# A gate's column sums: one fp32 matmul per step becomes one fp32r matmul on the high and low parts

## Chip, cores, metric

The kernel runs on one core of one Trainium2 chip. The metric is device microseconds for one execution. Three runs of the kernel before took 1857.21, 1858.81 and 1859.02 us, so the median is 1858.81 us.

## The reference

An attention over packed keys feeds a dense MLP, and its output feeds a mixture of experts. The change lies in the gate of that last part, so this is the piece that has to be seen (2304 tokens, 512 features, 8 experts):

```python
logits = x @ w_gate
logits = logits - logits.max()
P = np.exp(logits)
for _ in range(8):
    P /= P.sum(1, keepdims=True) + 1e-09
    P /= P.sum(0, keepdims=True) + 1e-09
    P *= N / E
out = np.zeros((N, D), dtype=np.float32)
for e in range(E):
    h = np.maximum(x @ w1[e], 0.0)
    ye = h @ w2[e]
    out += P[:, e:e + 1] * ye
```

`P` has one row per token and one column per expert. Eight times over, each row is divided by its sum and then each column by its sum.

## The kernel before

**Stages.** The first part (to about 420 us) is attention and the dense MLP. Then come the experts. The tokens stand in three groups of 512, 768 and 1024. The first group (about 420 to 780 us) is worked out in 32 units, one per quarter of an expert's hidden layer. While it runs, the weights of all experts are loaded, split into a high and a low part, and written back to memory for the two later groups, which take the rest of the time.

**A unit** (`unit`, L804) makes seven products of six matmuls each (`product`, L754, 256 columns) in three PSUM banks X, Z and Y. Between the products ScalarE copies a bank out (L815, L823, L826) and VectorE adds it to another bank (L817, L830, L833). `evac` then takes a finished bank out in two halves: ScalarE the high part (L761), VectorE the low part (L762). The second layer's matmuls (L784, 512 columns) of earlier units stand between the products. The names `hh`, `psc`, `psy`, `s` are the hidden layer's parts, the product banks, the second layer's banks and the copies.

**Weights beside it.** VectorE forms sums of weight blocks (L145 to L148, tile `wt`), ScalarE rounds a block to fp32r (L176, tile `w`), GpSimd subtracts to get the low part (L177), and SyncE writes both out (L181).

**The gate in it.** All 2304 rows of `P` lie in one tile of 128 partitions by 18 by 8. `balance` does one half step per call, and is called at fixed places of units 2 to 7: the 16 half steps take from 453 to 511 us. A row half step (`rows_step`, L712) is four VectorE instructions (L714 to L717) that divide each row by its sum, and a fifth (L719) that adds up the 18 rows of each partition to `cs`, 128 by 8. A column half step (`cols_step`, L722) adds `cs` over the partitions by a matmul with a matrix of ones (L724, a full fp32 matmul), after which VectorE makes the reciprocal (L726, L727) and multiplies `P` by it (L728).

**What sets the order.** The engines each run their own list of instructions strictly in order. The code is recorded in the order in which it is written, and a scheduler then orders each engine's list when the program is built, by durations that it assumes. So added or removed instructions can move others on the same engine. The matmul of a column step takes its PSUM bank from the four banks of the product banks (`ybank`, tag "c").

**Memory.** The tile pool `gc` holds the gate's small tiles. It is opened on the right side of the on-chip memory just before the pools of `s`, of half of `hb` (the second layer's operands of odd batches) and of `hh`, which are stacked next to it.

Of the kernel before, what the change touches and what calls it, by code (L numbers as in the profile page):

```python
# [10 lines left out]
F32 = mybir.dt.float32  # L11
F32R = mybir.dt.float32r
I32, U32, I64 = mybir.dt.int32, mybir.dt.uint32, mybir.dt.int64
AF = mybir.ActivationFunctionType
ALU = mybir.AluOpType
AX = mybir.AxisListType
# [3 lines left out]
T = B * S  # L20
DM, FF = 512, 2048
E, F = 8, 1024
# [10 lines left out]
EPS = 1e-9  # L33
# [5 lines left out]
def kernel(ctx: ExitStack, tc: tile.TileContext, qT, kT, v, pT,  # L39
                                     win, wout, wg, w1, w2, out):  # L40
    nc = tc.nc
# [14 lines left out]
    def pool(name, **kw):  # L56
        st, p = open_pool(name, **kw)
        ctx.push(st)
        return p

    const = pool("const", side="left")
# [13 lines left out]

    ident = const.tile([128, 128], F32, name="ident")
    make_identity(nc, ident)
    ones = const.tile([128, 128], F32, name="ones")
    nc.gpsimd.memset(ones, 1.0)


# [546 lines left out]
    for i, (f, c) in enumerate(seq):  # L628
        if i < 3:
            continue  # L630
        k = c + len(THIRDS) - len(BLOCKS[f])
# [45 lines left out]
    gc = pool("gc", side="right")  # L677
# [9 lines left out]
    def ybank():  # L687
        return psm.tile([128, 512], F32, tag="c", name="psy", bufs=4)
# [23 lines left out]
    def rows_step():  # L712
        rs = gc.tile([128, NT, 1], F32, tag="rs", name="rs")
        nc.vector.tensor_reduce(rs, P, axis=AX.X, op=ALU.add)  # L714
        nc.vector.tensor_scalar_add(rs, rs, EPS)
        nc.vector.reciprocal(rs, rs)
        nc.vector.tensor_tensor(P, P, rs.to_broadcast([128, NT, E]), op=ALU.mult)  # L717
        cs = gc.tile([128, E], F32, tag="cs", name="cs")
        nc.vector.tensor_reduce(cs, P.rearrange("p t e -> p e t"), axis=AX.X, op=ALU.add)  # L719
        return cs  # L720

    def cols_step(cs):  # L722
        ps = ybank()[:, :E]
        nc.tensor.matmul(ps, ones, cs, start=True, stop=True)  # L724
        cr = gc.tile([128, 1, E], F32, tag="cr", name="cr")
        nc.vector.tensor_scalar(cr[:, 0, :], ps, EPS, float(E) / T, op0=ALU.add, op1=ALU.mult)  # L726
        nc.vector.reciprocal(cr, cr)  # L727
        nc.vector.tensor_tensor(P, P, cr.to_broadcast([128, NT, E]), op=ALU.mult)  # L728

# [2 lines left out]
    def balance():  # L732

        n = steps["n"]
        if 0 <= n < 16:
            steps["n"] += 1
            if n % 2 == 0:
                steps["cs"] = rows_step()
            else:
                cols_step(steps["cs"])  # L740
# [510 lines left out]
```

## Time and profile before

| | |
|---|---|
| median of 3 runs | 1858.81 us |
| profiled execution, own time | 1860.79 us |
| its span, first to last instruction | 1858.9 us |
| PE busy | 1837.6 us (99%) |
| VectorE (DVE) busy | 1279.4 us (69%) |
| ScalarE (ACT) busy | 829.4 us (45%) |
| GpSimd (POOL) busy | 1047.0 us (56%) |
| mean granted clock of TensorE | 0.999 |

The profile comes from one execution, 1.98 us above the median of the runs; of that execution's own time, 1.9 us lie outside the span. PE is TensorE's matmuls, PEld its weight loads, which overlap the matmuls. Busy time of a matmul includes its way through the array, so PE can be called busy while one matmul follows another with a small hole. A fp32 matmul appears as two records, an fp32r matmul as one.

### The profile page before, as it was taken

How to read it: one execution, taken by the hardware profiler on the slowest of the kernel's cores; microseconds unless marked ns; L12 is line 12 of the kernel's file. 1: busy time of each engine (PE TensorE's matmuls, PEld its weight loads, DVE VectorE, ACT ScalarE, POOL GpSimd, SP SyncE). 2: the span in 40 equal slices, each digit the busy share in tenths (PEclk: the TensorE clock that was granted, in tenths of full speed). 3: DMA queues.
4: the chain of work that ended last, by engine and by line, in shares of the span. 5: the costliest groups of instructions: out<-in, count | busy, mean ns of one | idle time of the engine just before them, and what ended most of it. 6: DMA issues, size and time to landing. Idle time of an engine off the chain costs nothing.

```text
span 1858.9 us, 28526 instructions
## 1 busy us (share of the span) xinstructions
PE 1837.6 (99%) x10190; PEld 1663.2 (89%) x10190; DVE 1279.4 (69%) x2097; ACT 829.4 (45%) x1538; POOL 1047.0 (56%) x653
## 2 busy tenths in 40 slices
PE   8999999999999999999999999999999999999999
PEld 7899999998888898888888888888889999999998
DVE  4777777766766555588778877888775666666665
ACT  6667654644555555343333433333334323332323
POOL 3313322435688777278778777778764444444444
PEclk9999999999999999999999999999999999999999
DMA  7402211206789887767777787776788777788874
GB/s 277 159 27 77 69 46 47 103 2 229 252 317 325 299 271 255 243 219 257 234 249 233 233 267 233 238 238 228 248 307 268 276 258 266 258 245 265 267 251 148
DMA packets 166124, 403.55 MB, mean 217 GB/s; under 512 B 14192, under 2 KB 79712, under 8 KB 165984
## 3 DMA queue, kind: packets, MB, share of 16 engines
q1 hardware_dynamic: 131520, 346.15, 55.1%
q10 hardware_dynamic: 34464, 55.58, 9.8%
q8 instruction: 81, 1.33, 0.3%
q14 instruction: 59, 0.48, 0.1%
HBM read 273.96 MB, written 127.72 MB: 216 GB/s over the span
## 4 chain that ended last, share of the span: by engine, by line
PE 91%; DVE 3%; DMA 2%; issue 1%; ACT 1%; POOL 1%; SPq 0%; ACTq 0%; POOLq 0%; DVEq 0%
PE psc L754 35%; PE psx L1141 16%; PE psz L1141 12%; PE psy L430 11%; PE psy L784 7%; PE psh L411 6%; PE psh L364 1%; PE pp L270 1%; DMA raw<-win 1%; POOL w L177 1%; DMA raw<-w 1%; PE s L304 0%; PE s L238 0%; ACT w L176 0%; DMA kt<-kT 0%
## 5 line engine op out<-in xcount | busy, mean ns | idle before, releaser
L754 PE MATMUL psc<-xc,w 128*128 128x256 f32 (+2 forms) x4032 | 777.4, 335 | 2.3 <-ACT s L823 1.6
L754 PEld LDWEIGHTS psc<-xc,w 128*128 128x128 f32 x4032 | 666.3, 188 | 67.5 <-ACT s L823 1.8
L1117 POOL TENSOR_TENSOR hh<-hb,hh 128x1024 fp32r<-128x1024 f32 (+1 forms) x224 | 504.6, 2257 | 372.1 <-ACT hh L1116 314.4
L1116 ACT ACTIVATE hh<-hb 128x1024 fp32r<-128x1024 f32 (+1 forms) x224 | 213.8, 955 | 447.8 <-DVE hb L1114 197.8
L1141 PE MATMUL psx<-hh,wa 128*128 128x512 f32 (+1 forms) x1536 | 352.7, 362 | 0.0
L1141 PEld LDWEIGHTS psx<-hh,wa 128*128 128x128 f32 x1536 | 278.9, 188 | 30.2 <-ACT hh L1116 0.4
L1141 PE MATMUL psz<-hh,wa 128*128 128x512 f32 (+1 forms) x1152 | 261.9, 362 | 0.3 <-issue 0.3
L1141 PEld LDWEIGHTS psz<-hh,wa 128*128 128x128 f32 x1152 | 209.0, 188 | 23.2 <-issue 0.9
L430 PE MATMUL psy<-h,w 128*128 128x320 f32 (+2 forms) x1200 | 224.8, 331 | 0.2
L784 PE MATMUL psy<-w,hh 128*128 128x512 f32 x768 | 201.5, 395 | 3.9 <-ACT hh L761 3.3
L177 POOL TENSOR_TENSOR w<-raw,w 128x512 fp32r<-128x512 f32 (+1 forms) x128 | 157.9, 1255 | 76.9 <-ACT w L176 66.0
L1149 DVE TENSOR_TENSOR acc<-psx,acc 128x512 f32<-128x512 f32 (+1 forms) x248 | 152.1, 618 | 70.2 <-PE psx L1141 69.0
L430 PEld LDWEIGHTS psy<-h,w 128*128 128x128 f32 x1200 | 189.0, 188 | 12.2 <-ACT x L436 0.7
L1149 DVE TENSOR_TENSOR acc<-psz,acc 128x512 f32<-128x512 f32 (+1 forms) x184 | 112.6, 618 | 93.1 <-PE psz L1141 93.0
L1047 DVE SCALAR_TENSOR_TENSOR hb<-psc,gate 128x512 f32<-128x512 f32 (+1 forms) x256 | 157.3, 620 | 12.2 <-PE psc L754 7.3
L1021 POOL TENSOR_TENSOR wa<-rb,wa 128x512 fp32r<-128x512 f32 x80 | 132.6, 1666 | 49.9 <-ACT wa L1020 39.5
L784 PEld LDWEIGHTS psy<-w,hh 128*128 128x128 f32 x768 | 135.1, 189 | 27.8 <-ACT hh L761 4.6
L1114 DVE TENSOR_TENSOR hb<-hb 128x1024 f32<-128x1024 f32 (+1 forms) x96 | 133.5, 1390 | 28.9 <-POOL hh L1117 28.0
L411 PE MATMUL psh<-at,g 128*128 128x320 f32 (+2 forms) x768 | 123.4, 297 | 0.2 <-DVE r L417 0.2
L411 PEld LDWEIGHTS psh<-at,g 128*128 128x128 f32 x768 | 110.9, 189 | 4.3 <-DVE r L417 0.4
L177 POOL TENSOR_TENSOR w<-wt,w 128x512 fp32r<-128x512 f32 x64 | 83.7, 1316 | 47.8 <-ACT w L176 35.9
L129 POOL TENSOR_TENSOR ca<-ca,cc 128x512 int32<-128x512 int32 x28 | 36.7, 1311 | 102.6 <-ACT cc L128 94.1
(155 smaller groups left out, 1843.3 us busy)
## 6 DMA issues: line engine op xcount, KB each, us to landing
w<-kept_w SPq DMA_DIRECT2D x184, 512.0 KB, 4.8
kept_w<-wa SPq DMA_DIRECT2D x112, 512.0 KB, 4.6
wa<-kept_w SPq DMA_DIRECT2D x112, 512.0 KB, 4.8
kept_w<-w SPq DMA_DIRECT2D x96, 512.0 KB, 4.7
raw<-w ACTq DMA_DIRECT2D x58, 512.0 KB, 5.2
rb<-w ACTq DMA_DIRECT2D x64, 256.0 KB, 4.5
w<-kept_w SPq DMA_DIRECT2D x61, 256.0 KB, 4.3
raw<-win SPq DMA_DIRECT2D x16, 512.0 KB, 3.9
```

Of the source, the lines that this page charges most:

```text
L177: nc.gpsimd.tensor_tensor(w[:, 1, :n], t, w[:, 0, :n].bitcast(F32), op=ALU.subtract)
L411: nc.tensor.matmul(ps[:, u - begin:w - begin], gw[:, x, m * 128:(m + 1) * 128], at[:, y, g, u - b * S:w - b * S], start=(i == 0), stop=(i ...
L430: nc.tensor.matmul(ps[:, :n], w[:, x, d * 128:(d + 1) * 128], h[:, y, :], start=(i == 0), stop=(i == 11))
L754: last = nc.tensor.matmul(ps[:, :N], w[:, u, o + k * 128:o + (k + 1) * 128], x[v][:, k, :], start=(start and k + u + v == 0), stop=(k == 1 ...
L784: nc.tensor.matmul(ps, h[:, x, o:o + 128], w[:, y, :], start=(n % 4 + m + x + y == 0), stop=(n % 4 == 3 and m == 1 and x == 1), skip_group ...
L1021: nc.gpsimd.tensor_tensor(w[:, 1], src, w[:, 0].bitcast(F32), op=ALU.subtract)
L1047: nc.vector.scalar_tensor_tensor(HB[q][m, t][:, nn, :], src, 0.0, GATE[p, g // 4][:, t * N:(t + 1) * N], op0=ALU.max, op1=ALU.mult)
L1114: nc.vector.tensor_tensor(src, src, hb[MINUS[k]], op=ALU.subtract)
L1116: nc.scalar.activation(hi, src, AF.Copy)
L1117: nc.gpsimd.tensor_tensor(lo, src, hi.bitcast(F32), op=ALU.subtract)
L1141: nc.tensor.matmul(ps, A2[q, k][:, u, nn, d * 128:(d + 1) * 128], OPS[7 * q + k][v][:, nn, :], start=(first and nn + u + v == 0), stop=(nn ...
L1149: nc.vector.tensor_tensor(a, ps, a, op=ALU.add)
```

## The change

The eight sums of a partition are now split on ScalarE and VectorE into a part rounded to fp32r and the rest, side by side as 16 columns. One fp32r matmul with the same matrix of ones, now held as fp32r, adds both over the partitions. VectorE adds the two halves of the result as it takes them out of PSUM, and applies the constants in an instruction of its own.

```diff
@@ const @@
-    ones = const.tile([128, 128], F32, name="ones")
+    ones_r = const.tile([128, 128], F32R, name="ones")
+    ones = ones_r.bitcast(F32)
     nc.gpsimd.memset(ones, 1.0)
@@ rows_step, cols_step @@
         nc.vector.tensor_reduce(cs, P.rearrange("p t e -> p e t"), axis=AX.X, op=ALU.add)
-        return cs
-
-    def cols_step(cs):
-        ps = ybank()[:, :E]
-        nc.tensor.matmul(ps, ones, cs, start=True, stop=True)
+        parts = gc.tile([128, 2, E], F32R, tag="csr", name="parts")
+        nc.scalar.activation(parts[:, 0, :], cs, AF.Copy)
+        nc.vector.tensor_tensor(parts[:, 1, :], cs, parts[:, 0, :].bitcast(F32), op=ALU.subtract)
+        return parts
+
+    def cols_step(parts):
+        ps = ybank()[:, :2 * E]
+        nc.tensor.matmul(ps, ones_r, parts.rearrange("p k e -> p (k e)"), start=True, stop=True)
         cr = gc.tile([128, 1, E], F32, tag="cr", name="cr")
-        nc.vector.tensor_scalar(cr[:, 0, :], ps, EPS, float(E) / T, op0=ALU.add, op1=ALU.mult)
+        nc.vector.tensor_reduce(cr[:, 0, :], ps.rearrange("p (k e) -> p e k", e=E), axis=AX.X, op=ALU.add)
+        nc.vector.tensor_scalar(cr[:, 0, :], cr[:, 0, :], EPS, float(E) / T, op0=ALU.add, op1=ALU.mult)
         nc.vector.reciprocal(cr, cr)
         nc.vector.tensor_tensor(P, P, cr.to_broadcast([128, NT, E]), op=ALU.mult)
```

In the changed file the lines behind the first edit have numbers higher by 1, those behind the second by 5: the product is L759 there, the second layer L789, the high parts L766, the low parts L767. The new lines are L722 (ScalarE copy), L723 (VectorE subtraction), L728 (matmul), L730 (reduction out of PSUM) and L731 (constants). The tile `parts` takes 64 bytes of each partition, so the pools of `s`, `hh` and the odd `hb` begin 64 bytes lower than before, at addresses that are multiples of 64 bytes and no longer of 128.

The scheduler's lists are the same for GpSimd and SyncE, and on the other three engines up to the first column step. Between the first column step and unit 8 some instructions stand in another order. Three places follow, each with the list before and the list now.

VectorE, second column step; before, from the sums `cs` (L719) on; `wt` are the weight sums, `psc` the product banks:

```order
L719 TENSOR_REDUCE cs<-P 128x8
L145 TENSOR_TENSOR wt<-raw 128x256
L147 TENSOR_TENSOR wt<-raw 128x256
L830 TENSOR_TENSOR psc<-psc,s 128x256
L146 TENSOR_TENSOR wt<-wt,raw 128x256
L833 TENSOR_TENSOR psc<-psc,s 128x256
L148 TENSOR_TENSOR wt<-raw,wt 128x256
L762 SCALAR_TENSOR_TENSOR hh<-psc,hh 128x256 x2
L726 TENSOR_SCALAR cr<-psy 128x8
```

And now, where `parts` is the new tile:

```order
L720 TENSOR_REDUCE cs<-P 128x8
L835 TENSOR_TENSOR psc<-psc,s 128x256
L723 TENSOR_TENSOR parts<-cs,parts 128x8
L146 TENSOR_TENSOR wt<-raw 128x256
L148 TENSOR_TENSOR wt<-raw 128x256
L838 TENSOR_TENSOR psc<-psc,s 128x256
L147 TENSOR_TENSOR wt<-wt,raw 128x256
L767 SCALAR_TENSOR_TENSOR hh<-psc,hh 128x256
L149 TENSOR_TENSOR wt<-raw,wt 128x256
L767 SCALAR_TENSOR_TENSOR hh<-psc,hh 128x256
L730 TENSOR_REDUCE cr<-psy 128x8
L731 TENSOR_SCALAR cr<-cr 128x8
```

The addition into bank Z (L830, now L835) moved ahead of the first two weight sums, the subtraction stands behind it, and the addition into bank Y (L833, now L838) keeps its two weight sums in front.

ScalarE, third column step, before; `acc` is the copy of the second layer's first result:

```order
L790 ACTIVATE acc_4854<-psy 128x512 x2
L761 ACTIVATE hh<-psc 128x256
L111 DMA raw<-w 128x1024
L790 ACTIVATE acc_4854<-psy 128x512 x2
L823 ACTIVATE s<-psc 128x256
```

And now:

```order
L795 ACTIVATE acc_4854<-psy 128x512 x2
L766 ACTIVATE hh<-psc 128x256
L112 DMA raw<-w 128x1024
L722 ACTIVATE parts<-cs 128x8
L795 ACTIVATE acc_4854<-psy 128x512 x2
L828 ACTIVATE s<-psc 128x256
```

The new copy of `cs` stands behind two `acc` copies, a high part and the issue of a weight load; nothing else moved here.

TensorE, fourth column step, before; `xc_4182` holds the operands of the products behind which L830 and L833 come, `xc_4365` that of the unit's last product:

```order
L754 MATMUL psc<-xc_4182,w 128x256 x12
L784 MATMUL psy<-w,hh 128x512 x4
L754 MATMUL psc<-xc_4365,w 128x256 x6
L784 MATMUL psy<-w,hh 128x512 x14
L724 MATMUL psy<-cs,ones 128x8
L754 MATMUL psc<-xc_4181,w 128x256 x12
```

And now:

```order
L759 MATMUL psc<-xc_4182,w 128x256 x12
L759 MATMUL psc<-xc_4365,w 128x256 x6
L789 MATMUL psy<-w,hh 128x512 x18
L728 MATMUL psy<-parts,ones 128x16
L759 MATMUL psc<-xc_4181,w 128x256 x12
```

Four second-layer matmuls moved behind the unit's last product, which therefore follows at once on the product before it.

## Rows read from the trace of the kernel before

**Rows 1.** The page: busy time by engine; chain that ended last, by engine:

```profile
PE 1837.6 (99%) x10190; PEld 1663.2 (89%) x10190; DVE 1279.4 (69%) x2097; ACT 829.4 (45%) x1538; POOL 1047.0 (56%) x653
...
PE 91%; DVE 3%; DMA 2%; issue 1%; ACT 1%; POOL 1%; SPq 0%; ACTq 0%; POOLq 0%; DVEq 0%
```

**Rows 2.** Busy time of a window; waits of PE in it (us, times, longest):

```profile
453.00:512.00 59.00, 57.92 (x362) 51.64 (x362) 42.52 (x121) 30.00 (x72) 35.15 (x30) 1.00 0.70 249
...
PE psy L784 <- ACT hh L761: 0.9, 4, 0.3
```

**Rows 3.** Group by line, 453 to 512 us: xcount | busy, mean ns | idle:

```profile
L726 DVE TENSOR_SCALAR cr<-psy 128x8 f32<-128x8 f32 x8 | 1.3, 163 | 4.8 <-PE psy L724 4.8
```

**Rows 4.** Timeline, third column step: start us, us, engine, line [idle]:

```profile
468.74 1.53 PE L784 MATMUL psy<-w,hh 128*128 128x512 f32 x6
...
469.97 0.38 ACT L761 ACTIVATE hh<-psc 128x256 fp32r<-128x256 f32 x1
470.11 0.88 PE L754 MATMUL psc<-xc,w 128*128 128x256 f32 x6
...
470.38 0.42 DVE L762 SCALAR_TENSOR_TENSOR hh<-psc,hh 128x256 fp32r<-128x256 f32 x1 [1.41 <-ACT hh L761]
...
470.83 0.29 PE L724 MATMUL psy<-cs,ones 128*128 128x8 f32 x2
...
470.97 0.96 PE L754 MATMUL psc<-xc,w 128*128 128x256 f32 x6
```

**Rows 5.** Four small instructions by line: duration ns min/median/max, place:

```profile
L707 ACT ACTIVATE gm<-psy x1: 171/171/171, 447.4 to 447.4; 128x1 f32<-128x1 f32 x1
...
L701 DVE TENSOR_REDUCE grow<-psy x1: 278/278/278, 444.4 to 444.4; 1x1 f32<-1x128 f32 x1
...
L715 DVE TENSOR_SCALAR rs<-rs x8: 176/195/1260, 453.5 to 506.0; 128x18 f32<-128x18 f32 x8
...
L717 DVE TENSOR_TENSOR P<-P,rs x8: 307/494/1332, 455.1 to 506.5; 128x144 f32<-128x144 f32 x8
```

**Rows 6.** Timeline, first column step:

```profile
454.94 2.60 POOL L177 TENSOR_TENSOR w<-raw,w 128x512 fp32r<-128x512 f32 x2 [0.25 <-ACT w L176]
455.06 1.33 DVE L717 TENSOR_TENSOR P<-P,rs 128x144 f32<-128x144 f32 x1
...
456.65 0.40 DVE L719 TENSOR_REDUCE cs<-P 128x8 f32<-128x144 f32 x1
...
457.35 0.28 PE L724 MATMUL psy<-cs,ones 128*128 128x8 f32 x2
...
459.28 0.43 DVE L817 TENSOR_TENSOR psc<-psc,s 128x256 f32<-128x256 f32 x1 [0.86 <-PE psc L754]
```

**Rows 7.** Timeline, second column step:

```profile
461.68 0.44 DVE L719 TENSOR_REDUCE cs<-P 128x8 f32<-128x144 f32 x1
461.83 1.60 PE L754 MATMUL psc<-xc,w 128*128 128x256 f32 x12
462.82 0.43 DVE L830 TENSOR_TENSOR psc<-psc,s 128x256 f32<-128x256 f32 x1
463.27 0.29 PE L724 MATMUL psy<-cs,ones 128*128 128x8 f32 x2
463.72 1.20 PE L784 MATMUL psy<-w,hh 128*128 128x512 f32 x4 [0.17 <-ACT hh L761]
```

**Rows 8.** Timeline, fourth column step:

```profile
476.20 4.57 POOL L177 TENSOR_TENSOR w<-raw,w 128x256 fp32r<-128x256 f32 x4
...
478.62 0.44 DVE L719 TENSOR_REDUCE cs<-P 128x8 f32<-128x144 f32 x1
480.01 0.28 PE L724 MATMUL psy<-cs,ones 128*128 128x8 f32 x2
```

**Rows 9.** Weight loads and matmuls by line: duration ns min/median/max:

```profile
L500 PEld LDWEIGHTS pslg<-lx,wgs x56: 187/188/192, 361.2 to 418.0; 128*128 128x128 f32 x56
L1141 PE MATMUL psx<-hh,wa x1536: 333/389/497, 785.8 to 1853.6; 128*128 128x512 f32 x96, 128*128 128x384 f32 x96
```

## The prediction

> **What bounds the kernel now.** I read four things in this order: the page, the window in which the gate's steps run, the waits in it, and the timeline around single steps. The page says that TensorE (PE) is busy 99% of the span and makes up 91% of the chain that ended last [rows 1]. So a microsecond taken from or added to PE's list is one of the whole, unless a wait further on swallows it. In the window of the gate, 453 to 512 us, PE is busy 57.92 of 59.00 us, VectorE (DVE) 42.52, ScalarE 30.00 and GpSimd 35.15; the only wait of PE that is listed there is 0.9 us in four places, for ScalarE's high parts L761 [rows 2]. The gate's own instructions hide: VectorE's L726 waits for the matmul, 4.8 us in all [rows 3], but no row has PE waiting for the gate. To price the change I need what its matmul costs PE, and how long before that matmul its input is ready.
>
> **What the matmul costs now.** In the third step L724 starts at 470.83 and the next product at 470.97, so 0.14 us go to the two records of the fp32 matmul. The six products behind it take 0.96 us where the six before took 0.88 [rows 4], another 0.08. Together 0.22 us a step. In five of the eight steps (the first, third, fourth, sixth and seventh) a product follows like this, and the 0.22 us are PE's. In the other three the next instruction is a second-layer matmul that waits for ScalarE anyway: in the second step L724 starts at 463.27 and L784 at 463.72 with an idle 0.17 before it [rows 7]. Of these 0.45 us only 0.14 are the matmul's, so 0.31 us of slack swallow any saving.
>
> **What it costs then.** One fp32r matmul of 16 columns with its weight load is not in this trace. The nearest row is a product of 256 columns: twelve take 1.60 us [rows 7] and six 0.88 [rows 4], so six more cost 0.72 and one costs 0.12. From below the price is nothing, from above it is today's 0.22, if it goes through the array twice all the same. I take 0.12, the row's. The gain is 5 x 0.10 = 0.50 us, between 0 and 5 x 0.22 = 1.1.
>
> **What the longer way to it costs.** Between the sums `cs` and the matmul now stand a ScalarE copy and a VectorE subtraction. Neither is in the trace at this size. The nearest are a ScalarE copy of one column, 0.171 us [rows 5], and VectorE's L726 with 8 columns, 0.163 [rows 3]. A hand-over takes 0.03 (L761 ends at 470.35, L762 starts at 470.38 [rows 4]); I take that for all three. So the way is 0.17 + 0.17 + 0.09 = 0.43 us where both engines are free, and no less. What it does depends on the lead of today's `cs` on L724 and on what is queued ahead:
>
> - First step: `cs` ends at 457.05, L724 starts at 457.35 [rows 6]. The lead is 0.30, so PE waits at least 0.13. The subtraction would start at 457.28. GpSimd runs two subtractions from 454.94 for 2.60 us [rows 6], the second until 457.54. That holds VectorE back as GpSimd's run just before held L717 (1.33 us at 455.06, where 0.307 is its best [rows 5]): the matmul comes at 457.54 + 0.17 + 0.03 = 457.74 and the wait is 0.39. I take 0.39.
> - Second step, and alike the fifth and eighth: the lead is 463.27 - 462.12 = 1.15 us [rows 7], but the subtraction now stands behind the addition into Z (L830). That one needs the first six of the twelve products from 461.83, hence 461.83 + 0.88 + 0.03 = 462.74 at the earliest. With its 0.43 and the subtraction's 0.17 the matmul comes at 463.37, 0.10 late, inside the 0.31 us of slack above. The high part that L784 waits for comes no later, since L830 does not. Price 0. What is late next is the addition into Y behind two weight sums; the unit's last product needs its bank, and stands behind four second-layer matmuls that begin at 463.72 and take 1.20 us, which covers it.
> - Third step: the copy stands behind the high part L761, which ends at 470.35, the subtraction behind L762, which ends at 470.80; so the matmul comes at 471.03 instead of 470.83 [rows 4], 0.20 late. For the sixth step I take the same 0.20, though its matmul now stands behind more second-layer work, which could make it 0.
> - Fourth and seventh: the lead is 480.01 - 479.06 = 0.95 us. GpSimd's four subtractions from 476.20 take 4.57 us, 1.14 each [rows 8], so the third ends at 479.63. Held until then, the subtraction lets the matmul start at 479.83, before 480.01. Price 0.
>
> The waits add up to 0.39 + 2 x 0.20 = 0.79 us.
>
> **What comes behind the matmul.** L726 read PSUM and applied the constants in 0.16 us. Now a reduction out of PSUM (the nearest, L701, took 0.278) and the constants (L715, alike, 0.176 at the least) do it [rows 5]: 0.28 + 0.18 + 0.03 - 0.16 = 0.33 us more on VectorE per step. Behind it stands the addition L817, which today waits 0.86 us for PE [rows 6]. So even 0.39 + 0.33 is covered in the first step. In total VectorE gets 8 x (0.17 + 0.33) = 4.0 us more, against 59.00 - 42.52 = 16.5 us of idle time in the window [rows 2]. ScalarE gets 8 x 0.17 = 1.4 of its 29.0 idle us. No DMA is added; the weight loads that ScalarE issues move back by no more than a copy.
>
> [...] VectorE's L717, with both inputs in the on-chip memory, takes 0.307 us at best, 0.494 in the median and 1.332 at worst [rows 5]; the worst is the one that starts at 455.06 while GpSimd works from 454.94 [rows 6]. [...]
>
> **The sum.** -0.50 + 0.79 = +0.3 us. The profiled execution took 1860.79 us for a span of 1858.9, 1.98 above the median 1858.81. The difference holds for either, so I forecast 1858.81 + 0.3 = 1859.1 us. About 0.2% (3.7 us) is what a measurement of this kernel can tell from no change, so this is no change. Its own range goes from all gain and no wait, with the 1.08 us in which PE is idle in the window gone through the new order, 1858.81 - 1.1 - 1.1 = 1856.6, up to 1862.
>
> **Rivals.**
>
> *Slower through the lists.* Copy and subtraction stand at fixed places in lists that run in order: an evacuation ahead of them holds the matmul, and behind a late matmul PE has all its products. In the fourth step the unit's last product now follows at once on the one before it; it adds into a bank that VectorE must have read first (L833), and four second-layer matmuls no longer cover that. If PE waits for one more evacuation of 0.42 us [rows 4] in each step, that is 8 x 0.42 = 3.4 us. If GpSimd also holds VectorE in three of the eight by 1.332 - 0.307 = 1.02 us [rows 5], it is 6.5. The time is 1862.2 to 1865.3. It decides once PE stands 0.46 us per step on average. For it: GpSimd is busy 60% of the window. Against it: today PE waits 0.9 us in all here, and five of the leads can bear the longer way.
>
> *Slower or faster through addresses.* The 64 bytes of `parts` put the tiles `s`, `hh` and the odd `hb` on odd multiples of 64 bytes. All of the third part's L1141 matmuls stream `hh`. Weight loads show no difference: those of L500 read a tile whose slices begin on even and odd multiples of 64 by turns, and all take 187 to 192 ns [rows 9]. For streamed operands no row shows anything. [...] I put it at zero, the side of the row that was measured.
>
> *The matmul does not get cheaper.* If 16 columns in fp32r cost PE 0.22 us again, the gain of 0.50 goes and the time is 1859.6, still no change.
>
> *Faster.* If no wait appears, the new order removes PE's 1.08 us and the slack of 3 x 0.31 too, it is 1858.81 - 1.1 - 1.1 - 0.9 = 1855.7. Even that is within 0.2%, so faster needs addresses as well.
>
> **Chances.** The forecast with its own range 0.60, the matmul that costs the same 0.10, slower through the lists 0.15, slower through addresses 0.07, faster 0.08. So no change 0.70, slower 0.22, faster 0.08. The range leaves out the slow address case and the tails: 1856.0 to 1865.0.
>
> **What would show it.** Right: in the profile after, one record per step at L728, with about 0.12 us to the next product; a wait of PE before L728 of 0.2 to 0.4 us in the first and third step and none in the fourth and seventh; the rest of the span unchanged behind 540 us. Wrong: waits of PE before L728 or before the products of the fourth to sixth unit that add up to 3 us and more; or L1146 matmuls whose start-to-start time is no longer that of before, which would be the addresses.

## Result: 1.0% slower, and the profile after

The changed kernel takes 1876.62 us (median of 4 runs, 1875.41 to 1881.83); the kernel before took 1858.91 beside it. The ratio is 1.0103, 95% interval 1.0089 to 1.0116: 17.7 us slower. The forecast was 1859.1 with a range to 1865.0, so it was wrong. The profiled execution took 1881.83 us, its span is 1880.0.

The page after, answering [rows 1]:

```profile
PE 1855.4 (99%) x10182; PEld 1667.0 (89%) x10182; DVE 1294.6 (69%) x2113; ACT 832.0 (44%) x1546; POOL 1051.6 (56%) x653
...
PE 91%; DVE 4%; issue 1%; ACT 1%; POOL 1%; DMA 0%; ACTq 0%; POOLq 0%; DVEq 0%
```

PE has eight records less and 17.8 us more busy time: its matmuls got slower. Two rows say where. These are the matmuls by line (duration min/median/max, first and last start), of the kernel after; the column sums first:

```profile
L728 PE MATMUL psy<-parts,ones x8: 171/247/278, 461.1 to 517.5; 128*128 128x16 f32 x8
...
L1146 PE MATMUL psx<-hh,wa x1536: 331/392/504, 794.1 to 1874.7; 128*128 128x512 f32 x96, 128*128 128x384 f32 x96
```

And the column sums of the kernel before:

```profile
L724 PE MATMUL psy<-cs,ones x16: 170/215/256, 457.4 to 508.4; 128*128 128x8 f32 x16
```

From the first column sum to the last it took 51.0 us and takes 56.4: **+5.4 us in the gate**. From the first to the last matmul that streams `hh` into `psx` it took 1853.6 - 785.8 = 1067.8 us [rows 9] and takes 1080.6: **+12.8 us behind the gate**. Together 18.2, for 17.7 in the medians. The two spans differ by 21.1: another 3.7 us lie ahead of the first column sum (457.4 and 461.1), where the lists are the same and the granted clock from 440 to 450 us was 1.00 before and 0.83 after, and 0.8 are won back between the gate and the third part.

**In the gate**, the waits of PE from 455 to 545 us (total, times, longest), answering [rows 2], were 0.9 us for L761's high parts and little else. After:

```profile
PE psy L728 <- DVE parts L723: 2.3, 2, 1.7
PE psy L789 <- ACT hh L766: 0.6, 2, 0.3
PE psc L759 <- DVE psc L838: 0.5, 1, 0.5
PE psc L759 <- ACT s L828: 0.5, 1, 0.5
PE psy L789 <- DVE hh L767: 0.2, 1, 0.2
```

The longest is the third column step. The timeline after (start, duration, engine, line; idle before), from the second matmul on, answering [rows 4]:

```profile
467.22 0.25 PE L728 MATMUL psy<-parts,ones 128*128 128x16 f32 x1
...
469.21 2.55 POOL L178 TENSOR_TENSOR w<-wt,w 128x512 fp32r<-128x512 f32 x2 [8.17 <-ACT w L177]
469.33 0.16 DVE L730 TENSOR_REDUCE cr<-psy 128x8 f32<-128x16 f32 x1
469.53 1.00 DVE L731 TENSOR_SCALAR cr<-cr 128x8 f32<-128x8 f32 x1
...
470.80 1.12 DVE L733 TENSOR_TENSOR P<-P,cr 128x144 f32<-128x144 f32 x1
...
471.72 4.61 POOL L178 TENSOR_TENSOR w<-raw,w 128x256 fp32r<-128x256 f32 x4
...
472.50 1.32 DVE L716 TENSOR_SCALAR rs<-rs 128x18 f32<-128x18 f32 x1
...
474.36 0.85 DVE L718 TENSOR_TENSOR P<-P,rs 128x144 f32<-128x144 f32 x1
...
475.24 0.41 DVE L720 TENSOR_REDUCE cs<-P 128x8 f32<-128x144 f32 x1
...
475.92 0.43 DVE L723 TENSOR_TENSOR parts<-cs,parts 128x8 fp32r<-128x8 f32 x1
...
476.50 0.25 PE L728 MATMUL psy<-parts,ones 128*128 128x16 f32 x1 [1.73 <-DVE parts L723]
...
477.64 2.76 PE L789 MATMUL psy<-w,hh 128*128 128x512 f32 x6
```

The same instructions before, from the matmul at 463.27 [rows 7] on:

```profile
464.37 2.62 POOL L177 TENSOR_TENSOR w<-wt,w 128x512 fp32r<-128x512 f32 x2 [6.83 <-ACT w L176]
464.88 0.16 DVE L726 TENSOR_SCALAR cr<-psy 128x8 f32<-128x8 f32 x1
...
465.31 0.52 DVE L728 TENSOR_TENSOR P<-P,cr 128x144 f32<-128x144 f32 x1
...
466.83 0.19 DVE L715 TENSOR_SCALAR rs<-rs 128x18 f32<-128x18 f32 x1
...
467.36 0.49 DVE L717 TENSOR_TENSOR P<-P,rs 128x144 f32<-128x144 f32 x1
467.89 0.43 DVE L719 TENSOR_REDUCE cs<-P 128x8 f32<-128x144 f32 x1
```

Before, the sums were ready 5.05 us after the last matmul (463.27 to 468.32); after it is 8.43 (467.22 to 475.65). The new L731 takes 1.00 instead of nothing, beside GpSimd. All behind it slips against GpSimd's instructions, and L733, L716 and L718 now take 0.60, 1.13 and 0.36 longer beside them. These four add up to 3.1 of the 3.4 us. With copy and subtraction behind them the lead of 2.51 us that `cs` had on the third matmul is gone, and PE stands 1.73.

Then the clock falls. Busy time and granted clock (the number behind POOL) in three stretches of the kernel after:

```profile
470.00:476.50 6.50, 4.78 (x29) 4.02 (x27) 6.18 (x12) 4.44 (x12) 6.33 (x6) 1.00 0.66 243
476.50:480.30 3.80, 3.80 (x14) 3.22 (x15) 2.29 (x8) 2.48 (x6) 0.76 (x1) 0.58 0.85 302
480.30:486.00 5.70, 5.17 (x31) 4.50 (x30) 3.84 (x10) 2.08 (x5) 5.06 (x5) 0.98 0.85 294
```

Behind the wait 0.58 was granted. Six L789 take 2.76 us there where six took 1.53 [rows 4], six products 1.24 where 0.96: about 1.5 us. That the wait brought the fall is not shown; the first experiment has the same wait and no fall.

**Behind the gate**, matmuls by tile and columns (busy us, mean ns), after:

```profile
L759 PE MATMUL psc<-xc,w 128*128 128x512 f32 x1344 | 335.2, 391 | 0.3 <-DVE hb L1052 0.3
L759 PE MATMUL psc<-xc,w 128*128 128x384 f32 x1344 | 263.2, 336 | 0.0
L1146 PE MATMUL psx<-hh,wa 128*128 128x512 f32 x768 | 200.2, 394 | 0.0
L1146 PE MATMUL psx<-hh,wa 128*128 128x384 f32 x768 | 157.2, 336 | 0.0
L1146 PE MATMUL psz<-hh,wa 128*128 128x512 f32 x576 | 149.4, 394 | 0.0
```

And before:

```profile
L754 PE MATMUL psc<-xc,w 128*128 128x512 f32 x1344 | 332.2, 389 | 0.4 <-DVE hb L1047 0.4
L754 PE MATMUL psc<-xc,w 128*128 128x384 f32 x1344 | 261.5, 334 | 0.0
L1141 PE MATMUL psx<-hh,wa 128*128 128x512 f32 x768 | 195.4, 390 | 0.0
L1141 PE MATMUL psx<-hh,wa 128*128 128x384 f32 x768 | 157.2, 335 | 0.0
L1141 PE MATMUL psz<-hh,wa 128*128 128x512 f32 x576 | 145.9, 389 | 0.0
```

With nothing waited for, the 512-column matmuls that stream `hh` take 4.8 + 3.5 us more, 6.2 ns each, those of 384 columns nothing. The products between them, which stream `xc`, take 3.0 + 1.7 more: 13.0 in all.

### The profile page after: what moved, and what is told of

It reads as the page before. It is cut to its first block, busy times and chain, and to the rows that moved or that the text cites. A ratio compares the mean times of both kernels' runs of the same rounds, so it can differ in the third digit from the quotient of the medians.

```text
span 1880.0 us, 28547 instructions
## 1 busy us (share of the span) xinstructions
PE 1855.4 (99%) x10182; PEld 1667.0 (89%) x10182; DVE 1294.6 (69%) x2113; ACT 832.0 (44%) x1546; POOL 1051.6 (56%) x653
## 3 DMA queue, kind: packets, MB, share of 16 engines
q1 hardware_dynamic: 131520, 346.15, 54.8%
## 4 chain that ended last, share of the span: by engine, by line
PE 91%; DVE 4%; issue 1%; ACT 1%; POOL 1%; DMA 0%; ACTq 0%; POOLq 0%; DVEq 0%
PE psc L759 35%; PE psx L1146 16%; PE psz L1146 12%; PE psy L431 11%; PE psy L789 7%; PE psh L412 5%; PE psh L365 1%; PE pp L271 1%; PE s L305 0%; PE s L239 0%; POOL w L178 0%; DMA raw<-w 0%; PE pslg L501 0%; DVE wt L148 0%; DVE hh L767 0%
## 5 line engine op out<-in xcount | busy, mean ns | idle before, releaser
L759 PE MATMUL psc<-xc,w 128*128 128x256 f32 (+2 forms) x4032 | 783.5, 337 | 3.2 <-ACT s L828 2.1
L759 PEld LDWEIGHTS psc<-xc,w 128*128 128x128 f32 x4032 | 669.2, 189 | 73.9 <-ACT s L828 2.5
L1146 PE MATMUL psx<-hh,wa 128*128 128x512 f32 (+1 forms) x1536 | 357.4, 365 | 0.0
L789 PE MATMUL psy<-w,hh 128*128 128x512 f32 x768 | 203.1, 397 | 3.5 <-ACT hh L766 2.8
L789 PEld LDWEIGHTS psy<-w,hh 128*128 128x128 f32 x768 | 136.3, 190 | 27.1 <-ACT hh L766 3.6
```

The costliest lines, as they stand in the source:

```text
L759: last = nc.tensor.matmul(ps[:, :N], w[:, u, o + k * 128:o + (k + 1) * 128], x[v][:, k, :], start=(start and k + u + v == 0), stop=(k == 1 ...
L789: nc.tensor.matmul(ps, h[:, x, o:o + 128], w[:, y, :], start=(n % 4 + m + x + y == 0), stop=(n % 4 == 3 and m == 1 and x == 1), skip_group ...
L1146: nc.tensor.matmul(ps, A2[q, k][:, u, nn, d * 128:(d + 1) * 128], OPS[7 * q + k][v][:, nn, :], start=(first and nn + u + v == 0), stop=(nn ...
```

## Experiments

Two theories: addresses (12.8 us) and the gate's lists (5.4 us). The first kernel separates them, by taking 64 bytes from the pad in `gc`, so that `s`, `hh` and `hb` stand as before:

```diff
 # e1, on the changed kernel
-    gc.tile([128, 64], F32, name="gpad")
+    gc.tile([128, 48], F32, name="gpad")
```

> The changed kernel with the pad in pool gc cut from 64 to 48 columns: the lists of all engines are the same as in the changed kernel, and s, hh and hb lie where they lay before. Theory A (two causes: about 11 us from the addresses of hh, spread over the 512-column matmuls of L1146, and about 7 us from the new waits of the gate's window with the slower clock behind one of them): 1863 to 1867 us, L1146 with 512 columns back at 227 ns from start to start, and the window of 453 to 545 us as in the changed kernel. Theory B (the lists and waits did it all, the slower matmuls of the third part are a late effect of them): 1874 to 1878. Theory C (addresses did it all): 1857 to 1861.

Measured: 1863.81 us, ratio 1.0029 (1.0018 to 1.0040). Its column sums and its `hh` matmuls:

```profile
L728 PE MATMUL psy<-parts,ones x8: 172/247/278, 456.6 to 511.4; 128*128 128x16 f32 x8
...
L1146 PE MATMUL psx<-hh,wa x1536: 333/388/504, 786.5 to 1854.1; 128*128 128x512 f32 x96, 128*128 128x384 f32 x96
```

1067.6 us from first to last `hh` matmul: the address share is gone, and 5.0 us in the medians remain. The gate takes 54.8, 3.8 over before, with the same wait of 1.73 before L728, now at 472.00, but no fall of the clock (1.00) behind it in this execution:

```profile
472.00:476.00 4.00, 3.87 (x25) 3.41 (x25) 2.81 (x10) 2.74 (x7) 0.96 (x1) 1.00 0.90 311
```

This execution, at 1861.24, is one of the two fastest of its seven runs (1861.19 to 1866.36).

### Addresses

All of these are the kernel before with its lists unchanged; only pads differ.

```diff
 # e2 (80 columns), e4 (96), e10 (48), e6 (line left out)
-    gc.tile([128, 64], F32, name="gpad")
+    gc.tile([128, 80], F32, name="gpad")
 # e3: hh alone, between hq and hpa
+    pool("hpad", side="right").tile([128, 16], F32, name="hpad")
 # e5: everything on the left up, on the right down, by 128
+    const.tile([128, 32], F32, name="lpad")
-    edge.tile([128, 24], F32, name="edge")
+    edge.tile([128, 56], F32, name="edge")
 # e11: only the second weight pool up by 64, what follows by 256
+    pool("lpad1", side="left").tile([128, 16], F32, name="lpad1")
     wpools[1:] = [pool("wpb", side="left")] * 2
+    pool("lpad2", side="left").tile([128, 48], F32, name="lpad2")
```

> The kernel before with the pad in gc raised from 64 to 80 columns: same lists as before, s, hh and the odd hb 64 bytes lower, as in the changed kernel. Theory A: 1868 to 1872 us, with 233 ns from start to start for L1141 at 512 columns and 173 still at 384. Theory B: 1857 to 1861. Theory C: 1875 to 1878.

> The kernel before with a pad of 64 bytes between the pools hq and hpa: same lists, only hh 64 bytes lower, s and hb where they were. Theory A1 (the streamed operand hh alone pays): as the shift of all three, 1868 to 1872 us. Theory A2 (the writes and reads of s or hb pay, or any of the three in part): between 1859 and 1866, with L1141 at 227 ns.

> The kernel before with the pad in gc at 96 columns: same lists, s, hh and hb 128 bytes lower, again on multiples of 128. If what counts is the place within 128 bytes: 1857 to 1861 us and 227 ns for L1141 at 512 columns. If it is the distance to another tile, or the place within 256 bytes or more: 1865 to 1872 and 230 ns or more.

> The kernel before, same lists, with every tile moved by 128 bytes: those on the left side (weights w and wa, operands xc, sums) 128 up, those on the right (hh, s, hb, two xc) 128 down, so that all begin on a multiple of 256 bytes as against 128 over one. Theory R (what counts is the distance, modulo 256, between the operand that streams and the weights that load beside it; it is a multiple of 256 again): 1857 to 1862 us, L1141 at 227 ns with 512 columns. Theory P (the place itself counts, 128 over a multiple of 256 being the good one): L1141 and L754 at 233 ns and more, 1875 to 1900 us.

> The kernel before without the pad in gc: same lists, s, hh and hb 256 bytes higher. Theories R and P both: 1857 to 1862 us and 227 ns for L1141 at 512 columns, since 256 bytes are one period. If the period is 512 bytes or more: 230 ns or more and 1865 to 1880.

> The kernel before with hh, s and the odd hb 64 bytes higher instead of lower (lists unchanged). Theory that the distance between streamed operand and weights modulo 256 bytes sets the price: 64 above costs what 64 below cost, 232 to 234 ns for a matmul of 512 columns that streams hh, 1868 to 1872. Rival (a boundary that only a lower start crosses, or the half of a 128-byte piece in which a row starts): 227 ns, 1857 to 1861.

> The kernel before with hh where it was, and only the second weight pool (the weight tiles of the second and third part) 64 bytes higher; all else keeps its place modulo 256 bytes. Theory of the distance between streamed operand and weights: 232 to 234 ns for the 512-column matmuls of the third part that stream hh, and the products of the gate's stretch that load these weights (L759) rise as well; 1868 to 1880. Rival (distance between hh and other tiles, such as what VectorE or a DMA writes meanwhile): 227 ns and 1857 to 1861.

`d` is the distance from the weights `wa` to `hh` modulo 256 bytes (0 before); "stretch" is from the first to the last `hh` matmul of `psx`, "psx" the busy time of the 768 with 512 columns:

| kernel | d | stretch us | psx us | median us | ratio (95%) |
|---|---|---|---|---|---|
| e2: `s`, `hh`, odd `hb` -64 | -64 | 1080.4 | 200.2 | 1870.11 | 1.0065 (1.0050 to 1.0080) |
| e3: `hh` alone -64 | -64 | 1080.5 | 200.2 | 1870.55 | 1.0064 (1.0047 to 1.0081) |
| e4: as e2, -128 | 128 | 1081.8 | 199.9 | 1874.21 | 1.0086 (1.0071 to 1.0101) |
| e5: -128, weights +128 | 0 | 1067.5 | 195.5 | 1860.03 | 1.0004 (0.9995 to 1.0014) |
| e6: as e2, +256 | 0 | 1067.7 | 195.5 | 1859.59 | 1.0004 (0.9995 to 1.0014) |
| e10: as e2, +64 | 64 | 1077.6 | 198.2 | 1870.61 | 1.0061 (1.0045 to 1.0078) |
| e11: second weight pool +64 | -64 | 1083.5 | 200.3 | 1875.41 | 1.0089 (1.0074 to 1.0104) |

The rows for two of them, e3 and then e11:

```profile
L1142 PE MATMUL psx<-hh,wa 128*128 128x512 f32 x768 | 200.2, 395 | 0.0
L1142 PE MATMUL psx<-hh,wa 128*128 128x384 f32 x768 | 157.2, 336 | 0.0
```

```profile
L1143 PE MATMUL psx<-hh,wa 128*128 128x512 f32 x768 | 200.3, 396 | 0.0
L1143 PE MATMUL psx<-hh,wa 128*128 128x384 f32 x768 | 159.2, 338 | 0.0
```

e2 repeats the address share without the change: 12.6 us. e3 gives it to `hh` alone. e4 refutes what I thought then, that a start off a multiple of 128 bytes costs: 128 lower costs more still, above either range that I gave. e5 puts both operands on other places at the same distance and costs nothing, and 256 bytes (e6) cost nothing. e11 leaves `hh` where it was and moves the weights: the price is there again, as expected. e10's time came as expected, but not from the price that was expected: its "psx" is 2.8 us up where -64 has 4.8, and its products between are 5.9 up. So in the third part the price depends on the distance, modulo 256 bytes, between `hh` and what lies in the second weight pool.

It is no rule for every matmul. In the first group the second layer streams `w` with `hh` as its weights, also 512 columns. e2 puts these two 64 bytes apart as well, and they take no longer. And the products of the first group that load from e11's moved pool were expected to rise and did not. Before and e2, then before and e11:

```profile
L784 PE MATMUL psy<-w,hh 128*128 128x512 f32 x768 | 201.5, 395 | 3.9 <-ACT hh L761 3.3 <-DVE acc L794 0.4
L784 PE MATMUL psy<-w,hh 128*128 128x512 f32 x768 | 201.4, 395 | 4.1 <-ACT hh L761 3.4 <-DVE acc L794 0.4
L754 PE MATMUL psc<-xc,w 128*128 128x256 f32 x1344 | 184.1, 283 | 1.9 <-ACT s L823 1.6 <-ACT s L815 0.3
L756 PE MATMUL psc<-xc,w 128*128 128x256 f32 x1344 | 183.7, 282 | 1.1 <-ACT s L825 0.9 <-ACT s L817 0.3
```

Nor do a matmul's own two operands explain the products of the third part. Nearly all of them keep `xc` and `w` at distance 0 in every kernel here, and yet they take 4.7 us more in e3, where only `hh` moved, and 4.1 in e11. How the distance acts stays open.

What the distance does not settle is the size. With `d` at -64 by either operand the 512 columns cost the same, but the 384 columns cost 2.0 us only in e11; at +64 (e10) the 512 columns cost 2.8 where -64 costs 4.8. e11's pool also holds the even `hb`, from which `hh` is made, so that it is `wa` that counts is inferred from the matmul's operands and not shown.

### The gate's lists

Each has the addresses of before: e8, e9 and e12 by a smaller pad, as e1; e7 has no `parts` and needs none. The main lines of each edit:

```diff
 # e7: sums rounded to fp32r, low parts left out; one matmul, tail as before
+        cs = gc.tile([128, E], F32R, tag="cs", name="cs")
+        nc.tensor.matmul(ps, ones_r, cs, start=True, stop=True)
 # e8, on e1: two accumulating matmuls, tail as before
+        for k in range(2):
+            nc.tensor.matmul(ps, ones_r, parts[:, k, :], start=(k == 0), stop=(k == 1))
 # e9, on e1: no L731; T/E goes into L733, 1e-9 left out
-        nc.vector.tensor_scalar(cr[:, 0, :], cr[:, 0, :], EPS, float(E) / T, op0=ALU.add, op1=ALU.mult)
+        nc.vector.scalar_tensor_tensor(P, P, float(T) / E, cr.to_broadcast([128, NT, E]), op0=ALU.mult, op1=ALU.mult)
 # e12, on e1: constants out of PSUM first, then the reduction, out of SBUF
+        nc.vector.tensor_scalar(c2, ps, EPS / 2, float(E) / T, op0=ALU.add, op1=ALU.mult)
+        nc.vector.tensor_reduce(cr[:, 0, :], c2.rearrange("p (k e) -> p e k", e=E), axis=AX.X, op=ALU.add)
```

> The kernel before with the sums cs written as fp32r by the reduction itself and added by one fp32r matmul of 8 columns: same lists, same addresses, no copy, no subtraction, no addition of halves. The low parts of the sums are left out. It measures the gain of the matmul alone: by the prediction's term 0.10 us in each of five steps, 1858.3 (within 1856.5 to 1860); if the matmul costs the same, 1858.8; the step's own share in the trace is 0.12 us to the next product in place of 0.22.

> The realigned changed kernel (e1) with the high and the low part as two fp32r matmuls of 8 columns that add up in PSUM: VectorE's tail is again L726 alone, with the constants, and the copy and the subtraction stay in front. If the longer tail behind the matmul makes the waits (0.33 us more of VectorE in each step): 1858 to 1861 us. If the longer way in front makes them: 1862 to 1866, as e1.

> The change with its addresses put back to those of before, and with the constants applied elsewhere: behind the matmul stand only the reduction out of PSUM and the reciprocal; the factor T/E goes into the product with P (one scalar_tensor_tensor in place of a tensor_tensor), and the addition of 1e-9 is left out. Tail theory (the constants' small instruction from SBUF to SBUF, which GpSimd holds, makes the gate window late): 1858.3 to 1860.0, no wait of PE above 1 us before L728. Rival (the way in front of the matmul, copy and subtraction): 1861 to 1865 as with the realigned change, which took 1863.8.

> The change with its addresses put back to those of before, and its tail in the other order: the constants are applied on the way out of PSUM (16 columns), then the reduction adds the halves, out of SBUF. As many instructions as in the change. If GpSimd's hold of the small SBUF-to-SBUF instruction with constants is what delays (1.00 us in the third step of the changed kernel), and a reduction is not held: 1858.5 to 1860.5. Rival (one instruction more, of whatever kind): 1861.5 to 1865.

| kernel | first to last column sum, us | wait in the third step | median us | ratio (95%) |
|---|---|---|---|---|
| before | 51.0 | 0 | 1858.8 to 1859.5 | |
| e7: matmul alone | 50.5 | 0 | 1858.45 | 0.9998 (0.9988 to 1.0007) |
| e8: with the way in front | 52.7 | 1.06 | 1859.45 | 1.0003 (0.9993 to 1.0012) |
| e9: and the reduction | 53.0 | 0.49 | 1860.82 | 1.0004 (0.9995 to 1.0014) |
| e12: and the constants, out of PSUM | 53.3 | 0.43 | 1862.40 | 1.0017 (1.0007 to 1.0026) |
| e1: the constants from SBUF | 54.8 | 1.73 | 1863.81 | 1.0029 (1.0018 to 1.0040) |

e12 has as many instructions as e1 and, but for the exchanged pair and the place of one weight rounding on ScalarE, the same lists. The two tails by line (duration min/median/max), e1 and then e12:

```profile
L730 DVE TENSOR_REDUCE cr<-psy x8: 161/173/175, 456.9 to 513.5; 128x8 f32<-128x16 f32 x8
...
L731 DVE TENSOR_SCALAR cr<-cr x8: 170/610/1011, 457.1 to 513.7; 128x8 f32<-128x8 f32 x8
```

```profile
L731 DVE TENSOR_SCALAR c<-psy x8: 166/174/175, 460.0 to 515.2; 128x16 f32<-128x16 f32 x8
...
L732 DVE TENSOR_REDUCE cr<-c x8: 169/171/172, 460.2 to 515.4; 128x8 f32<-128x16 f32 x8
```

The same constants took 0.17 us out of PSUM in all eight steps and up to 1.01 from SBUF to SBUF; the reduction from SBUF took 0.17 in all eight. In the third step both run beside GpSimd: e1's L731 from 465.02 for 1.01 us with GpSimd's two subtractions from 464.71 for 2.56, e12's L731 and L732 from 467.89 for 0.17 each with GpSimd's two from 467.78 for 2.62. On the trace e12 wins back 1.5 of e1's 3.8 us, and the long wait falls from 1.73 to 0.43: that share goes with the constants' time beside GpSimd. But e12's 1862.40 is above the 1858.5 to 1860.5 that the hold alone gave it, in the range of its rival (one instruction more), and below e1 by 1.4 with intervals that overlap: the hold explains the long wait, not all of the loss. e9 likewise has no wait above 0.5 and ends 0.8 above its expectation, between its two ranges. e8 ended in the range of the tail, not of the way in front. Over the kernel before as it ran beside them, the medians are +0.5 (e8), +1.3 (e9), +2.9 (e12) and +5.0 us (e1).

The 2.3 us of the gate that are left in e12 go with waits of up to 0.5 us each, before L728, for L839 and for a copy `s`. The longer way and the new order bring these together, and no run here parts them. e8 does not either: its lists moved further, and in six of its eight steps products stand between its two column sums, which start 0.9 to 2.0 us apart, so its tail starts later. Its third step:

```profile
474.04 0.27 PE L729 MATMUL psy<-parts,ones 128*128 128x8 f32 x1 [1.06 <-ACT parts L722]
474.17 0.96 PE L759 MATMUL psc<-xc,w 128*128 128x256 f32 x6
474.97 0.17 PE L729 MATMUL psy<-parts,ones 128*128 128x8 f32 x1
```

The wait of 1.06 there comes behind an L716 that started at 470.80 beside GpSimd's subtractions and took 1.13.

No kernel here beats the one before: e7, which leaves out the low parts, is within the noise of it.

## Why the prediction was wrong

Two steps failed: the tail was called covered, and the address term was put at zero.

- **What bounds it**: right. Every microsecond lost is one on PE's list.
- **The matmul, -0.50**: the size was right where the operand is ready. In the gate e7, with 8 columns, gives -0.5 (51.0 to 50.5), too little to show in its median. In the changed kernel the next product starts 0.03 us behind L728 in the fourth step, but 0.10 to 0.13 in the first, third, sixth and seventh (third: 476.50 and 476.60), against 0.14 [rows 4]: less is saved there.
- **Waits, +0.79**: in the first step 0.39 and in the sixth 0.20 were forecast, and none is listed. In the third 0.20 was forecast and **1.73** measured; in the seventh none was forecast, and the other wait before L728 in the list (2.3 less 1.7, 0.6) stands there.
- **The tail, +0.33 per step, hidden.** "So even 0.39 + 0.33 is covered in the first step" was the step that failed in the gate. I looked for its cover on VectorE up to the next addition (L817), in one step, and kept today's time for the next `cs`. But the tail lies on the way from one matmul to the next. And its size was wrong: I priced the constants by L715's least, 0.176, though the same row reads 195 in the median and 1260 at worst [rows 5]. Measured 170/606/1009.
- **GpSimd's hold on VectorE** was applied to instructions with two inputs only. The constants, with one input, took up to 1.01 us from SBUF to SBUF beside GpSimd (L731 in e1) and 0.17 out of PSUM (L731 in e12), the reduction from SBUF 0.17 (L732 in e12). L715, also with one input, had shown it in the kernel before: 1.26 us at 453.46, with GpSimd's two subtractions from 452.69 to 454.69, where 0.176 is its least [rows 5]. This told against the change and was left out.
- **Rival "slower through the lists"** (3.4 to 6.5 us, chance 0.15): it came, 5.4 us. One of its places came as described: in the unit of the fourth step the last product waits 0.5 us for L838. Not foreseen was the clock's fall, about 1.5 us; without it e1 lost 3.8 in the gate.
- **Rival "slower through addresses"** (chance 0.07): it came too, 12.8 us. "I put it at zero, the side of the row that was measured" is the step that cost most. The row was one of weight loads (L500); for streamed operands I had said that no row shows anything, and put zero all the same. The pattern was also another: not odd multiples of 64 (e4 pays on a multiple of 128) but the distance to the second weight pool, 6.2 ns on 512 columns and nothing on 384, and 4.7 us on the products.

## What to carry to other kernels

A new small tile is also an address change for every pool stacked behind it (12.8 us here): restore the addresses with a pad before judging the edit. Price a small VectorE instruction by the spread of its row, not its least, when GpSimd works beside it (L715: 0.176 to 1.26 us), and take constants out of PSUM on the way (0.17 us in e12, up to 1.01 from SBUF in e1). In a loop whose steps feed each other, what stands behind one matmul stands in front of the next.

## What the runs showed that I had not expected

The distance modulo 256 bytes between `hh`, which the third part streams, and the second weight pool is worth 11 to 16 us in the medians here. The stretch takes 1067.5 to 1068.1 us at distance 0, and 1077.6 to 1083.5 at 64, 128 and 192 bytes. And a wait of 1.73 us was followed by a granted clock of 0.58 over 3.8 us in one execution, while the same wait in e1's was followed by none of it; what decides between them stays open.
